# Four small moves in a TensorE-bound attention and MLP kernel: a weight transfer in halves, later numerators, two matmuls ahead of a spread, an epsilon on TensorE

## Chip, cores, metric

One core of one Trainium2 chip. The metric is the device time of one execution in microseconds (us), the median of several runs. The kernel before takes 294.08 us. The experiments ran later, in three rounds on three chips, each beside the kernel before, whose medians there were 293.73, 293.66 and 293.97; so compare ratios, and absolute times only within a round.

## The reference, cut to what matters

```python
# linear attention: 8 batches, 8 heads, 576 tokens, 64 wide; phi(x) = elu(x) + 1
q_p, k_p = phi(q), phi(k)
kv  = einsum('bhsd,bhse->bhde', k_p, v)
z   = sum(k_p, axis=2)
num = einsum('bhsd,bhde->bhse', q_p, kv)
den = einsum('bhsd,bhd->bhs', q_p, z)[..., None] + 1e-06
x   = (num / den) as 4608 tokens x 512
# two dense layers
h = x @ w_in                 # 512 x 2048
out = (h - tanh(h)) @ w_out  # 2048 x 512
```

## The kernel before

The 4608 tokens pass in nine chunks of 512. A chunk's first layer is 64 matmuls (line L366), its second layer 64 (L387), and the attention of the next batch is laid between them. During chunk 0 the weights still arrive, and batch 1 is prepared with four spare PSUM banks (`side`); PSUM is the memory that matmuls write to, and this kernel deals it out in banks of 512 columns. The attention divides a numerator (`num`) by a denominator (`den`). `num1` writes five tiles in turn into the banks that `side` hands out, directly after `a_den` has taken one, so its **fourth** tile (pair 2) falls on the bank of den. `1/den` is spread over partitions by matmuls (L240 for batch 0, L354 for batch 1), whose result VectorE multiplies with num into xT.

```python
def a_den(b, banks, parts=range(4)):
    ps = banks()[:, 0:J * 16]
    for t in range(4) if b == 0 else ():          # epsilon by TensorE, batch 0 only
        nc.tensor.matmul(ps[32 * t:32 * t + 32], eps[:, 0:32], one[:, 0:J * 16], start=True, stop=False)
    ...                                           # 16 matmuls into ps (L276)
    if b > 0:
        den = rpool.tile([128, J * 16], F32, name="den")
        nc.vector.tensor_scalar(den, ps, 1e-6, None, ALU.add)    # L281
    else:
        den = ps
    nc.vector.reciprocal(rden, den)               # L285
# cut: a_split, four VectorE operations on rden, the last one is L298
# cut: load_wo(g) loads w_out rows 512 g to 512 g + 512, one quarter

# chunk 0
side = Banks([4, 5, 6, 7])
def num1():
    sub["ns"] = new_ns(1)
    for p in (NP, 0, 1, 2, 3):
        a_num_copy(1, sub["ns"], p, side)         # matmul L320/L317, then a ScalarE copy L346/L344
s2[7].append(lambda: (a_qT_pe(1, 0, side), a_kv(1, side), a_qT_pe(1, 1, side)))
s2[8].append(lambda: b0_scale_rest(side))
s2[9].append(lambda: (a_den(1, side), num1(), a_split(1)))
s2[11].append(lambda: spread1(0))                 # L354
...
order = [((0, 0), (0, 1)), ((2, 0), (2, 1), (0, 2), (0, 3), (2, 2), (2, 3)),
         [(p, fi) for p in (1, 3) for fi in range(4)]]
for n, part_ in enumerate(order):
    if n == 1:
        open2()                                   # second spread L240, then the scalings L244
    ...
# later chunks: num of the next batch after second-layer step 11 + p (chunk 1)
s2[(11 if c == 1 else 9) + p].append(lambda p=p: a_num(n1, p))
```

Of the kernel before, what the change touches and what calls it, by code (L numbers as in the profile page):

```python
# [18 lines left out]
def kernel(  # L19
# [9 lines left out]
    nc = tc.nc  # L29
# [4 lines left out]
    NP = H // 2  # L34
# [79 lines left out]
    def load_wo(g):  # L114
        nc.gpsimd.dma_start(out=w_out_sb[:, 4 * g:4 * g + 4, :],
                            in_=moe_w_out[512 * g:512 * g + 512, :].rearrange("(ko ki) f -> ki ko f", ki=128))
# [150 lines left out]
    def a_den(b, banks, parts=range(4)):  # L267

        kz, qT = kz_t[b], qT_t[b]
        ps = banks()[:, 0:J * 16]  # L270
        for t in range(4) if b == 0 else ():
            nc.tensor.matmul(ps[32 * t:32 * t + 32], eps[:, 0:32], one[:, 0:J * 16], start=True, stop=False)
        for n, p in enumerate((0, 2, 1, 3)):
            if n in parts:
                for t in range(4):
                    nc.tensor.matmul(ps[32 * t:32 * t + 32], kz[:, p // 2, p % 2, 128:160],  # L276
                                     qT[:, p % 2, :, p // 2, 16 * t:16 * t + 16],
                                     start=(n == 0 and b > 0), stop=(n == NP - 1))
        if b > 0:
            den = rpool.tile([128, J * 16], F32, name="den")  # L280
            nc.vector.tensor_scalar(den, ps, 1e-6, None, ALU.add)  # L281
        else:
            den = ps
        rden = rpool.tile([128, J * 16], F32, name="rden")
        nc.vector.reciprocal(rden, den)  # L285
        rden_t[b] = rden
# [37 lines left out]
    def a_num(b, p):  # L324
        rdb = rdb_t[b]
        ps = num_mm(b, p, attn)
        if p < NP:
            nc.vector.tensor_mul(  # L328
                xT[:, p, S * b:S * b + 512].rearrange("p (j t c) -> p j t c", j=8, t=4),
                ps.rearrange("p j (t c) -> p j t c", t=4),  # L330
                rdb[:, p, :, 0:8, :].rearrange("p t j c -> p j t c"))
        else:
            nc.vector.tensor_mul(
                xT[:, :, S * b + 512:S * b + 576].rearrange("p a (t c) -> p a t c", t=4),
                ps[:, 0:NP, :].rearrange("p a (t c) -> p a t c", t=4), rdb[:, :, :, 8, :])
# [29 lines left out]
    def l1mm(c, fi, h, p, n):  # L365
        nc.tensor.matmul(h, w_in_sb[:, 2 * (p % 2) + p // 2, fi * 128:(fi + 1) * 128], xT[:, p, c * 512:(c + 1) * 512],  # L366
                         start=(n == 0), stop=(n == NP - 1))
# [17 lines left out]
    def l2mm(gT, o, i, f0, f1):  # L385
        for fi in range(f0, f1):
            nc.tensor.matmul(o, gT[:, fi, i * 128:(i + 1) * 128], w_out_sb[:, fi, :],  # L387
                             start=(fi == 0), stop=(fi == NF - 1))
# [30 lines left out]
        nc.gpsimd.memset(v_b[i][:, 2], 1.0)  # L419
    nc.gpsimd.memset(vp[:, :, :, 128:136], 1.0)  # L420
    load_v(1)
    load_wo(2)
    load_wo(3)

    nc.vector.memset(mask, 0.0)
# [78 lines left out]
    for c in range(NC):  # L504
        gT = gpool.tile([128, NF, 512], BF16, name="gT")
        n1, n2 = c + 1, c + 2
        s1 = {i: [] for i in range(16)}
        s2 = {i: [] for i in range(16)}
        if c == 0:
            side = Banks([4, 5, 6, 7])  # L510
            sub = {}

            def spread1(h):
                sub["bp"] = a_spread_pe(1, 4, (2 * h, 2 * h + 1))
                for p in (2 * h, 2 * h + 1):
                    a_scale(1, p, sub["ns"], sub["bp"], 144 * (p % 2))
# [4 lines that stand above are left out]
                    a_num_copy(1, sub["ns"], p, side)  # L521

            s1[11].append(lambda: a_kphi(1, 0))
            s1[13].append(lambda: a_kphi(1, 1))
            s2[3].append(lambda: a_qphi(1, 0))
            s2[4].append(lambda: (a_qphi(1, 1), load_q(2), load_k(2), load_v(2)))
            s2[0].append(prepare)
# [5 lines that stand above are left out]
            qs, ks = [], []  # L533

            def exp2(pieces, src, store, name, i):
                pieces.append(phi_pieces(2, src, store, name, i))
                pieces[i][0]()

            def rest2(f):
                f[1]()  # L540
                f[2]()

            s2[11].append(lambda: (exp2(qs, q_t, qp_t, "qp", 0), rest2(qs[0])))
            s2[12].append(lambda: exp2(qs, q_t, qp_t, "qp", 1))
            s2[13].append(lambda: (spread1(1), exp2(ks, k_t, kp_t, "kp", 0), rest2(qs[1]), a_qT_dma(2)))
            s2[14].append(lambda: rest2(ks[0]))
        elif n1 < B:
            s1[8 if c == 1 else 5].append(lambda: a_kv_cols(n1, attn))
            s1[10 if c == 1 else 8].append(lambda: (a_den(n1, attn), a_spread(n1)))
            for p in range(NP + 1):  # L550
                s2[(11 if c == 1 else 9) + p].append(lambda p=p: a_num(n1, p))
        if c == 1:
            s1[1].append(lambda: a_kphi(2, 1))
            s1[3].append(lambda: (a_vp(2, 0), a_vp(2, 1)))
        if c >= 1 and n2 < B:

            s1[0].append(lambda: (gate(qT_t[n1]), load_k(n2), load_q(n2), load_v(n2)))
            d = 2
            s2[d].append(lambda: a_kphi(n2, 0))
            s2[d + 2].append(lambda: a_kphi(n2, 1))  # L560
            s2[d + 4].append(lambda: a_qphi(n2, 0))
            s2[d + 6].append(lambda: (a_qphi(n2, 1), a_qT_dma(n2)))
            for i in range(2):
                s2[14 + i].append(lambda i=i: a_vp(n2, i))
        if c == 0:

            first = Banks([4, 5, 6, 7, 0, 1, 2, 3])
            hs = [ps_all[:, n, :] for n in range(4)]
            order = [((0, 0), (0, 1)), ((2, 0), (2, 1), (0, 2), (0, 3), (2, 2), (2, 3)),
                     [(p, fi) for p in (1, 3) for fi in range(4)]]  # L570
            seen = [0] * 4
            for n, part_ in enumerate(order):
                if n == 1:
                    open2()
                for x in range(2 if n == 0 else 0):
                    for p, fi in part_:
                        nc.tensor.matmul(hs[fi][:, 256 * x:256 * x + 256], w_in_sb[:, 0, fi * 128:(fi + 1) * 128],
                                         xT[:, p, 256 * x:256 * x + 256], start=(x == 0), stop=False)
                        seen[fi] = 1
                for p, fi in part_ if n else ():  # L580
                    l1mm(c, fi, hs[fi], p, seen[fi])
                    seen[fi] += 1
            for fi in range(4):
                l1act(fi, hs[fi], gT)
        for fi in range(4 if c == 0 else 0, NF):
            h = first() if c == 0 else dense()
            for p in range(NP):
                l1mm(c, fi, h, p, p)
            if c == 0:
                l1act(fi, h, gT)  # L590
            elif fi % 2:
                n = dense.order[(dense.n - 1) % 6]
                l1act2(fi - 1, ps_all[:, n - 1:n + 1, :], gT)
            for f in s1[fi]:
                f()
        os_ = {}
        for s in range(16):

            (g, i) = divmod(s, 4) if c == 0 else (s % 4, s // 4)
            if g == 0:  # L600
                os_[i] = ps_all[:, i, :] if c == 0 else dense()
            if c == NC - 1 and i == 3:

                if g == 0:
                    o2 = dense()
                    for o, f in ((os_[i], slice(0, 384)), (o2, slice(384, DM))):
                        for fi in range(NF):
                            nc.tensor.matmul(o[:, f], gT[:, fi, 384:512], w_out_sb[:, fi, f],
                                             start=(fi == 0), stop=(fi == NF - 1))
                        evac(c, i, o, f.start, f.stop)  # L610
                continue
            l2mm(gT, os_[i], i, 4 * g, 4 * g + 4)
            if g == 3:
                evac(c, i, os_[i])
            for f in s2[s]:
                f()
# [30 lines left out]
```

## Time and profile before

| | kernel before |
|---|---|
| time, median | 294.08 us |
| span in the trace | 291.8 us |
| TensorE busy | 97%, granted clock 1.00 throughout |
| VectorE, ScalarE busy | 60%, 48% |

How to read it: the kernel is bound by TensorE nearly everywhere, so only delays of TensorE's own starts count. The lines for three such delays are in the prediction below, with the reason why busy shares do not show them. The timeline of the kernel before has the num matmuls of batch 1 and ScalarE's copies of them:

```profile
43.36 1.03 PE L317 MATMUL ps_all<-qT,kz 128*128 128x512 bf16 x4
43.83 2.06 ACT L344 COPY ns<-ps_all 128x512 f32<-128x512 f32 x4
```

The columns of a timeline are start and duration in us, engine, line, operation, tiles, and count. Four matmuls in 1.03 us is 3 x 0.216 + 0.38: they run without any gap.

### The profile page before, as it was taken

Reading aid. Unit: us, or ns where it says so; the run is one execution under the profiler, and the core shown is the slowest. Engines: PE = TensorE matmul, PEld = TensorE weight load, DVE = VectorE, ACT = ScalarE, POOL = GpSimd, SP = SyncE. Lnnn points to the kernel's source line nnn. Section 1 sums busy time; section 2 is a strip of 40 time slices with the busy share of each in tenths; the row PEclk is TensorE's granted clock in tenths of the full one; section 3 lists DMA queues with packets and bytes.
Section 4 is the critical chain, followed back from the end, with each engine's and each line's share of the span. In section 5 each row is a group of like instructions: output and inputs, shape, how many; then the busy total and the mean of one; then the engine's idle time right before and its main releaser. Section 6 shows DMA issues by size and latency. Waiting matters only on the chain.

```text
span 291.8 us, 4476 instructions
## 1 busy us (share of the span) xinstructions
PE 284.2 (97%) x1775; PEld 134.5 (46%) x1803; DVE 174.8 (60%) x266; ACT 139.7 (48%) x168; POOL 33.1 (11%) x55
## 2 busy tenths in 40 slices
PE   8999999999999999999999999999999999999994
PEld 3544464454454444544444445444444444444443
DVE  4759958987458674776478637865581457106600
ACT  4838638846254733465345534751551155126411
POOL 8673030110030003000300030000000000000000
PEclk9999999999999999999999999999999999999999
DMA  6999999998989668955795579766117310130032
GB/s 96 198 204 212 208 207 213 214 168 145 253 158 159 170 131 135 200 139 127 134 223 131 120 137 196 144 142 139 32 34 168 73 36 0 42 84 20 0 74 72
DMA packets 39077, 38.94 MB, mean 133 GB/s; under 512 B 16336, under 2 KB 33808, under 8 KB 38288
## 3 DMA queue, kind: packets, MB, share of 16 engines
q0 software_dynamic: 17552, 18.35, 39.0%
q1 hardware_dynamic: 21344, 20.17, 30.5%
q8 instruction: 14, 0.23, 0.3%
q10 hardware_dynamic: 160, 0.13, 0.1%
q14 instruction: 7, 0.06, 0.1%
HBM read 43.91 MB, written 9.55 MB: 183 GB/s over the span
## 4 chain that ended last, share of the span: by engine, by line
PE 75%; DMA 18%; POOL 2%; issue 1%; SPq 1%; DVE 1%; ACT 1%; DVEq 0%; POOLq 0%
PE ps_all L366 37%; PE ps_all L387 32%; DMA w_out_sb<-in_moe_w_out_dram 6%; DMA w_in_sb<-in_moe_w_in_dram 3%; DMA rdb<-ds 3%; DMA out_dram<-osb 2%; PE ps_all L199 2%; DMA kraw<-in_k_dram 2%; PE ps_all L317 2%; DMA ds<-rden 1%; PE ps_all L276 1%; POOL v L419 1%; ACT osb L396 1%; SPq L401 0%; POOL qraw L90 0%
## 5 line engine op out<-in xcount | busy, mean ns | idle before, releaser
L366 PE MATMUL ps_all<-xT,w_in_sb 128*128 128x512 bf16 x558 | 126.5, 380 | 0.9 <-issue 0.2
L387 PE MATMUL ps_all<-w_out_sb,gT 128*128 128x512 bf16 x548 | 126.2, 380 | 0.7
L373 DVE TENSOR_TENSOR gT<-ps_all,th 128x1024 bf16<-128x1024 f32 x64 | 77.9, 1218 | 59.7 <-ACT th L372 59.7
L372 ACT ACTIVATE th<-ps_all 128x1024 f32<-128x1024 f32 x64 | 65.5, 1023 | 57.0 <-PE ps_all L366 46.4
L366 PEld LDWEIGHTS <-w_in_sb 128*128 128x128 bf16 x574 | 55.0, 98 | 66.0
L387 PEld LDWEIGHTS <-gT 128*128 128x128 bf16 x560 | 54.1, 98 | 64.7 <-issue 0.6
L396 ACT COPY osb<-ps_all 128x512 f32<-128x512 f32 (+1 forms) x36 | 20.8, 582 | 72.3 <-PE ps_all L387 55.9
L328 DVE TENSOR_TENSOR xT<-ps_all,rdb 128x512 bf16<-128x512 f32 x24 | 16.3, 689 | 13.7 <-PE ps_all L317 11.2
L134 ACT ACTIVATE e<-qraw 128x1152 bf16<-128x1152 bf16 x16 | 18.5, 1161 | 7.3 <-DMA qraw<-in_q_dram 7.3
L134 ACT ACTIVATE e<-kraw 128x1152 bf16<-128x1152 bf16 x15 | 17.4, 1162 | 0.1
L136 DVE TENSOR_TENSOR qp<-e,r 128x1152 bf16<-128x1152 bf16 x16 | 12.1, 758 | 7.8 <-ACT e L134 7.0
L136 DVE TENSOR_TENSOR kp<-e,r 128x1152 bf16<-128x1152 bf16 x15 | 11.4, 758 | 7.9 <-ACT e L134 7.0
L383 POOL COPY g<-qT 1x1 bf16<-1x1 bf16 x5 | 0.9, 182 | 119.7 <-DMA qT<-qp 119.7
L378 DVE TENSOR_TENSOR gT<-ps_all,th 128x512 bf16<-128x512 f32 x16 | 10.3, 686 | 2.3 <-ACT th L377 1.7
L377 ACT ACTIVATE th<-ps_all 128x512 f32<-128x512 f32 x16 | 9.2, 598 | 4.4 <-PE ps_all L366 3.2
L444 PE MATMUL ps_all<-zero 128*128 128x512 bf16 x29 | 9.3, 487 | 1.2 <-DVE zero L405 1.2
L317 PE MATMUL ps_all<-qT,kz 128*128 128x512 bf16 x28 | 10.1, 380 | 0.1
L135 DVE TENSOR_SCALAR r<-qraw 128x1152 bf16<-128x1152 bf16 x16 | 7.3, 453 | 1.9 <-DMA qraw<-in_q_dram 1.9
L199 PEld LDWEIGHTS <-kp 64*128 64x128 bf16 x216 | 6.4, 94 | 2.5 <-issue 2.5
L285 DVE RECIPROCAL rden<-den 128x144 f32<-128x144 f32 x7 | 7.4, 1052 | 0.2
L199 PE MATMUL ps_all<-vp,kp 64*128 64x136 bf16 x216 | 7.4, 220 | 0.0
L394 DVE COPY osb<-ps_all 128x128 f32<-128x128 f32 x1 | 0.3, 291 | 11.6 <-DMA out_dram<-osb 11.6
(84 smaller groups left out, 123.0 us busy)
## 6 DMA issues: line engine op xcount, KB each, us to landing
out_dram<-osb SPq DMA_DIRECT2D x70, 128.0 KB
rdb<-ds SPq DMA_DIRECT2D x12, 576.0 KB
kraw<-in_k_dram POOLq DMA_DIRECT2D x7, 576.0 KB, 7.1
qraw<-in_q_dram POOLq DMA_DIRECT2D x7, 576.0 KB, 9.2
v<-in_v_dram POOLq DMA_DIRECT2D x7, 576.0 KB, 11.9
w_out_sb<-in_moe_w_out_dram POOLq DMA_DIRECT2D x4, 512.0 KB, 16.0
w_in_sb<-in_moe_w_in_dram POOLq DMA_DIRECT2D x6, 256.0 KB, 8.6
qraw<-in_q_dram POOLq DMA_DIRECT2D x2, 288.0 KB, 4.4
```

The costliest lines, as they stand in the source:

```text
L134: return (lambda: nc.scalar.activation(e, x, AF.Exp), lambda: nc.vector.tensor_scalar(r, x, 0.0, 1.0, ALU.max, ALU.add), lambda: nc.vector ...
L136: lambda: nc.vector.tensor_tensor(y, e, r, ALU.min))
L199: nc.tensor.matmul(ps[hg][:, i, :], kp[r, i, j].rearrange("p h d -> p (h d)"), vp[r, i, j, :], start=(j == 0), stop=(j == J - 1))
L317: nc.tensor.matmul(ps, kz[:, p // 2, p % 2, 0:128], qT[:, p % 2, 0:8, p // 2, :], start=True, stop=True)
L328: nc.vector.tensor_mul(xT[:, p, S * b:S * b + 512].rearrange("p (j t c) -> p j t c", j=8, t=4), ps.rearrange("p j (t c) -> p j t c", t=4), ...
L366: nc.tensor.matmul(h, w_in_sb[:, 2 * (p % 2) + p // 2, fi * 128:(fi + 1) * 128], xT[:, p, c * 512:(c + 1) * 512], start=(n == 0), stop=(n ...
L372: nc.scalar.activation(th, h, AF.Tanh)
L373: nc.vector.tensor_sub(gT[:, fi:fi + 2, :], h, th)
L378: nc.vector.tensor_sub(gT[:, fi, :], h, th)
L387: nc.tensor.matmul(o, gT[:, fi, i * 128:(i + 1) * 128], w_out_sb[:, fi, :], start=(fi == 0), stop=(fi == NF - 1))
L396: nc.scalar.copy(osb[:, f0:f1], o[:, f0:f1])
L444: nc.tensor.matmul(ps_all[:, 0, :], zero[:, 0:128], zero, start=True, stop=True)
```

## The change

Its intent is to remove four waits: (1) for the third w_out quarter, by loading it in halves; (2) ahead of the second 1/den spread of batch 0, by laying two matmuls there; (3) for the 1/den chain of batch 1, by letting TensorE add the epsilon as it does for batch 0; (4) for the broadcast of 1/den of batch 2, by taking its num later.

```diff
 def a_den(...):
-        for t in range(4) if b == 0 else ():
+        for t in range(4) if b < 2 else ():
             nc.tensor.matmul(ps[32 * t:32 * t + 32], eps[:, 0:32], one[:, 0:J * 16], start=True, stop=False)
 ...
-                                     start=(n == 0 and b > 0), stop=(n == NP - 1))
-        if b > 0:
+                                     start=(n == 0 and b > 1), stop=(n == NP - 1))
+        if b > 1:
 ...
-    load_wo(2)
+    for n in range(2):
+        nc.gpsimd.dma_start(out=w_out_sb[:, 8 + 2 * n:10 + 2 * n, :],
+                            in_=moe_w_out[1024 + 256 * n:1280 + 256 * n, :].rearrange("(ko ki) f -> ki ko f", ki=128))
 ...
-                s2[(11 if c == 1 else 9) + p].append(lambda p=p: a_num(n1, p))
+                s2[min(12 + p, 15) if c == 1 else 9 + p].append(lambda p=p: a_num(n1, p))
 ...
-            order = [((0, 0), (0, 1)), ((2, 0), (2, 1), (0, 2), (0, 3), (2, 2), (2, 3)),
+            order = [((0, 0), (0, 1)), ((2, 0), (2, 1)), ((0, 2), (0, 3), (2, 2), (2, 3)),
                      [(p, fi) for p in (1, 3) for fi in range(4)]]
-                if n == 1:
+                if n == 2:
                     open2()
 ...
             # first layer of chunk 2: pairs 0 and 1 of its first two blocks, then pairs 2 and 3
+            if c == 2 and fi == 1:
+                for two in (0, 2):
+                    for f, o in ((0, ...), (1, h)):
+                        for p in (two, two + 1):
+                            l1mm(c, f, o, p, p)
 ...
-            l2mm(gT, os_[i], i, 4 * g, 4 * g + 4)
+            if c == 0 and g == 2:        # four blocks with the first half, then four with the second
+                for n in (2 * i, 2 * i + 1):
+                    f = 8 + 2 * (n // 4)
+                    l2mm(gT, os_[n % 4], n % 4, f, f + 2)
```

More of the change, by code (lines that the diff above doesn't have):

```diff
@@ L586 @@
             h = first() if c == 0 else dense()
-            for p in range(NP):
-                l1mm(c, fi, h, p, p)
+            if c == 2 and fi == 1:
+                for two in (0, 2):
+                    for f, o in ((0, ps_all[:, dense.order[(dense.n - 2) % 6], :]), (1, h)):
+                        for p in (two, two + 1):
+                            l1mm(c, f, o, p, p)
+            elif c != 2 or fi > 1:
+                for p in range(NP):
+                    l1mm(c, fi, h, p, p)
             if c == 0:
@@ L611 @@
                 continue
-            l2mm(gT, os_[i], i, 4 * g, 4 * g + 4)
+            if c == 0 and g == 2:
+                for n in (2 * i, 2 * i + 1):
+                    f = 8 + 2 * (n // 4)
+                    l2mm(gT, os_[n % 4], n % 4, f, f + 2)
+            else:
+                l2mm(gT, os_[i], i, 4 * g, 4 * g + 4)
             if g == 3:
```

## The prediction

> **What bounds the kernel now.** I read the page first, then the chain in order of time, then the timeline around the places that the diff touches. The page:
>
> ```profile
> PE 284.2 (97%) x1775; PEld 134.5 (46%) x1803; DVE 174.8 (60%) x266; ACT 139.7 (48%) x168; POOL 33.1 (11%) x55
> PEclk9999999999999999999999999999999999999999
> L366 PE MATMUL ps_all<-xT,w_in_sb 128*128 128x512 bf16 x558 | 126.5, 380 | 0.9 <-issue 0.2
> L387 PE MATMUL ps_all<-w_out_sb,gT 128*128 128x512 bf16 x548 | 126.2, 380 | 0.7
> ```
>
> TensorE is the bound over the whole span, at full clock. But "97% busy" hides waits: a matmul's span is 380 ns, while in a dense run the next starts 216 ns after it, so a wait of up to some 160 ns is covered by the pipeline's tail. So I work with starts, not idle time. A group of n such matmuls lasts (n-1) x 0.216 + 0.38 us; its last start is its end less 0.38. Some records are missing (both rows should have 576), which shows as a pitch of 432 ns with a weight load in its middle; I count none of those as a wait. A walk over all PE starts with this rule leaves, after the first 18 us, three real stalls, and the diff aims at each. There are no others above 0.1 us beyond the fixed 0.1 us at each change of the array's tile shape.
>
> Stall one, the third w_out quarter, in the chain in order of time and in the timeline:
>
> ```profile
> 23.05 17.84 DMA w_out_sb<-in_moe_w_out_dram
> ...
> 40.20 0.68 PE L164 MATMUL ps_all<-ident,qp 128*128 128x128 bf16 x9
> 40.93 1.02 PE L387 MATMUL ps_all<-w_out_sb,gT 128*128 128x512 bf16 x3
> ```
>
> The ninth transpose starts at 40.20 + 0.68 - 0.22 = 40.66 (one lasts 0.22), its pitch is 0.055, so L387 could start at 40.71. It starts at 40.93, just after the transfer ends at 40.89: a stall of 0.22 us.
>
> Stall two, the 1/den chain of batch 1 on VectorE:
>
> ```profile
> 41.91 1.03 PE L387 MATMUL ps_all<-w_out_sb,gT 128*128 128x512 bf16 x4
> 42.87 0.43 PE L276 MATMUL ps_all<-qT,kz 128*32 128x144 bf16 x16
> 43.35 0.31 DVE L281 TENSOR_SCALAR den<-ps_all 128x144 f32<-128x144 f32 x1 [0.82 <-PE ps_all L276]
> 43.70 1.05 DVE L285 RECIPROCAL rden<-den 128x144 f32<-128x144 f32 x1
> 44.23 1.89 PE L387 MATMUL ps_all<-w_out_sb,gT 128*128 128x512 bf16 x8
> 45.73 0.37 DVE L298 SCALAR_TENSOR_TENSOR w<-t,part,u 128x144 bf16<-128x144 bf16 x1
> 46.16 0.30 PE L354 MATMUL ps_all<-w,sel 32*128 32x144 bf16 x8
> ```
>
> The last L387 before L354 starts at 44.23 + 1.89 - 0.38 = 45.74. A change to small tiles costs 0.31 from start to start (41.91 + 1.03 - 0.38 = 42.56 to 42.87), so L354 could start at 46.05; it starts at 46.16, after L298 ends at 46.10. Stall: 0.11 us.
>
> Stall three, num of batch 2:
>
> ```profile
> 69.80 7.88 DMA rdb<-ds
> 77.80 0.70 DVE xT L328
> 78.54 0.38 PE ps_all L317
> ...
> 77.41 1.03 PE L387 MATMUL ps_all<-w_out_sb,gT 128*128 128x512 bf16 x4
> ```
>
> Num 0 to 4 alternate between two banks, so num 2 (78.54) waits until L328 has read num 0, and that waits for the broadcast that lands at 77.68. The last L387 starts at 77.41 + 1.03 - 0.38 = 78.06; num 2 could follow at 78.28. Stall: 0.27 us.
>
> **What the Trainium skill says.** "TensorE: Matmul & The Clock Gate", section "Wait — 56ns, not 53.3ns?", gives 215.7 ns between 512-column matmuls and 55.6 ns at 128 columns on a warm array; the trace agrees (216 and 55). The same page, section "The mechanism" of Part 3, says that matmuls on different 32-wide tiles run at once, some 4 ns apart; here sixteen L276 take 0.43 us in all, so it agrees. "PSUM — Partial Sum Buffer", section "PSUM bank collisions raise a hardware error", asks for guards by bank and quadrant, not by address; the trace agrees that the second spread (L240) starts only when L244 has stopped reading other columns of the same banks. "DMA: Bandwidth & Descriptors", section "Queues, rings and completion order", says that each engine consumes its ring's descriptors in order, so a first half comes before a second; no run shows this for halves yet.
>
> **The change part by part.** (1) *w_out quarter in halves.* No byte is added, one more issue on GpSimd (0.74 us for a whole quarter). It delays only the last quarter's issue, and GpSimd idles 13.8 us afterwards. In the transfer view from 20 to 50 us:
>
> ```profile
> DMA packets 5924, 6.25 MB, mean 208 GB/s; under 512 B 225, under 2 KB 5920, under 8 KB 5920
> ```
>
> A quarter of 0.52 MB takes 2.5 us, a half 1.26, so the first half should land near 40.89 - 1.26 = 39.6 and the second near 40.9. The matmuls are reordered so that the first eight use the first half alone; the second half is needed only some 2.5 us after 40.7. The stall goes: -0.22.
>
> (2) *Two matmuls of the second pair ahead of the second spread.*
>
> ```profile
> 15.64 1.35 DVE L244 TENSOR_TENSOR xT<-ns,ps_all 128x256 bf16<-128x256 f32 x3 [0.50 <-PE ps_all L240]
> 16.12 0.71 PE L577 MATMUL ps_all<-xT,w_in_sb 128*128 128x256 bf16 x4
> 17.05 0.73 PE L240 MATMUL ps_all<-rden,sel 32*128 32x128 f32 x16 [0.22 <-DVE xT L244]
> 17.70 2.70 PEld L366 LDWEIGHTS <-w_in_sb 128*128 128x128 bf16 x14
> 17.91 1.28 DVE L244 TENSOR_TENSOR xT<-ns,ps_all 128x512 bf16<-128x512 f32 x2 [0.92 <-PE ps_all L240]
> ```
>
> TensorE could go on at 16.67 (the last half-width matmul starts at 16.56 and takes 0.11) and idles until 17.05, until the third L244 ends at 16.99. The intent is to fill that gap. But the two moved matmuls read the xT rows that this same third L244 writes: in the built program the wait passes from the spread to them. So the gap stays. They run at 17.05 and 17.26, the spread then starts 0.31 after the latter (a change of tile shape that was hidden in the idle time), at 17.57, against 17.05 + 0.43 = 17.48 if the order cost nothing: +0.09. The scaling of pair 1 follows 0.52 later: 17.91 + 0.52 + 0.69 = 19.12 at its end, and the matmul that needs it can start at 19.18. TensorE's first matmul after the spread stood at 17.72 (the second weight load of L366; that matmul's record is missing, the one at 17.93 is the next). Now it stands 0.52 later and four precede pair 1: 17.72 + 0.52 + 4 x 0.216 = 19.10, so +0.07. Before, it came at 17.72 + 6 x 0.216 = 19.01 with 18.60 ready. Sum: **+0.16**, a loss.
>
> (3) *Epsilon of batch 1 by PE.* Four more small matmuls run at once: a row of four takes about 0.06 (sixteen start within 0.21), +0.06. L281 goes; the reciprocal starts 0.35 earlier less 0.06, and reads the bank directly, which batch 0 does already in 1.06 us. The chain ends 0.29 sooner, more than the 0.11 stall: -0.11. Net -0.05. The rest of the 0.29 is slack.
>
> (4) *Num of batch 2 later by one step, the last two together.* No instruction is added. Num 2 now comes four matmuls later, at about 79.15 where num 0 was read at 78.50: -0.27. The price to check is at the end, since chunk 2 of the first layer needs num 3's xT, and one vp copy (0.45) now stands ahead of its scaling. By the old clock num 3 would run at 80.20, its scaling from 80.64 to 81.33. Hence the new order of the first eight L366: pairs 0 and 1 of both blocks (80.55 to 81.41), then pair 2, then pair 3 at 81.63. It is in time by 0.25. Num 4 needs the bank of num 2 free at 80.26 and comes at 80.44. No new wait.
>
> Sum: -0.22 + 0.16 - 0.05 - 0.27 = -0.38 us on a TensorE-bound program, so nearly all of it arrives at the end: 294.08 - 0.38 = **293.7 us**.
>
> **The rivals.** (a) Part 2 works as meant, and its idle 0.38 is filled: then the sum is -0.38 - 0.16 - 0.38, or 293.2. Against it speaks that both readers wait for the same L244. (b) A new wait takes the place of the third stall: pair 3's scaling slips by more than its 0.25 of slack behind the vp copy. Then up to 0.27 is given back: 293.95. For it, VectorE's queue there is in order; against it, the sums above. (c) The w_out wait only moves: with TensorE later by 0.16 from part 2, the whole quarter would have been met at 40.87, so splitting would be worth just 0.06. That is already in the sum, since the two together are worth 0.06; if the half landed no earlier than the quarter, they would be worth 0: 293.75. (d) The transfers' timing differs from run to run, so that the two transfer stalls are typically larger or smaller than in the one trace: plus or minus 0.2.
>
> **Range and chances.** The three runs before spread over 0.43 us (293.9 to 294.33), and the effect is of that size. From (a) to (b), with some tenths for the chip: 293.2 to 294.1. Two per cent is 5.9 us, and all known stalls after the start together are 0.6: faster 0.01, same 0.98, slower 0.01.
>
> **What would show it right or wrong.** In the profile after: L387 follows the last transpose within 0.06 us (part 1); two L366 start near 17.05, the spread near 17.57, and the gap after the four half-width matmuls still ends when L244 does (part 2); L354 follows L387 by 0.31 (part 3); every L317 follows L387 by 0.22 and the first eight L366 of chunk 2 stand 0.216 apart (part 4). I am wrong if the moved L366 start well before 17.0, if a gap above 0.1 us appears near 81 us, or if the sum of start delays does not match the change in span.

## The result, and the profile after

The changed kernel takes 293.85 us (median of five runs, 293.51 to 294.21). The ratio to the kernel before is 0.9997, with a 95% interval of 0.9982 to 1.0011: no difference that the runs can tell.

The page after, in the lines that answer to those of before:

```profile
PE 286.1 (98%) x1807; PEld 134.7 (46%) x1807; DVE 174.7 (60%) x265; ACT 139.7 (48%) x168; POOL 33.7 (12%) x56
L387 PE MATMUL ps_all<-w_out_sb,gT 128*128 128x512 bf16 x560 | 127.5, 379 | 0.0
```

TensorE's busy time rose by 1.9 us while the span stayed, but that is no added work: 1807 matmul records stand here, only 1775 before, and the change adds four. The weight loads, 1803 before and 1807 after, differ by just these four: 28 matmul records are missing before and none after. So again the starts decide. The three stalls of before are gone or changed. The timeline after, at the second spread of batch 0 (part 2):

```profile
15.98 0.71 PE L580 MATMUL ps_all<-xT,w_in_sb 128*128 128x256 bf16 x4
16.90 0.59 PE L366 MATMUL ps_all<-xT,w_in_sb 128*128 128x512 bf16 x2 [0.22 <-DVE xT L244]
17.43 0.73 PE L240 MATMUL ps_all<-rden,sel 32*128 32x128 f32 x16
18.29 1.29 DVE L244 TENSOR_TENSOR xT<-ns,ps_all 128x512 bf16<-128x512 f32 x2 [1.44 <-PE ps_all L240]
```

The last half-width matmul (256 columns, L577 before, L580 after) starts at 15.98 + 0.71 - 0.27 = 16.42. The two moved L366 follow at 16.90, 0.49 later by the unrounded starts; before, it was the spread that followed, after the same 0.49. The gap is not filled, the wait has only passed to the moved matmuls.

The timeline after, around the transposes, den and num of batch 1 (parts 1 and 3):

```profile
40.21 0.68 PE L164 MATMUL ps_all<-ident,qp 128*128 128x128 bf16 x9
40.72 1.03 PE L387 MATMUL ps_all<-w_out_sb,gT 128*128 128x512 bf16 x4
42.73 0.42 PE L276 MATMUL ps_all<-qT,kz 128*32 128x144 bf16 x16
43.21 1.06 DVE L285 RECIPROCAL rden<-ps_all 128x144 f32<-128x144 f32 x1 [0.88 <-PE ps_all L276]
43.22 0.59 PE L317 MATMUL ps_all<-qT,kz 128*128 128x512 bf16 x2
44.32 0.59 PE L317 MATMUL ps_all<-qT,kz 128*128 128x512 bf16 x2 [0.51 <-DVE rden L285]
44.75 1.89 PE L387 MATMUL ps_all<-w_out_sb,gT 128*128 128x512 bf16 x8
45.25 0.37 DVE L298 SCALAR_TENSOR_TENSOR w<-t,part,u 128x144 bf16<-128x144 bf16 x1
46.57 0.30 PE L354 MATMUL ps_all<-w,sel 32*128 32x144 bf16 x8
```

L387 now follows the last transpose at once (40.67 to 40.72): part 1 worked. But the four num matmuls no longer run together. Two run, then TensorE stands still until the reciprocal ends at 43.21 + 1.06 = 44.27. The second pair could have started at 43.22 + 2 x 0.216 = 43.65 and starts at 44.32: a **new stall of 0.67 us**. The chain of splits ends at 45.62, nearly a microsecond ahead of L354: its gain is not used.

And at num of batch 2 (part 4):

```profile
78.69 1.03 PE L387 MATMUL ps_all<-w_out_sb,gT 128*128 128x512 bf16 x4
79.56 0.38 PE L317 MATMUL ps_all<-qT,kz 128*128 128x512 bf16 x1
80.97 4.26 PE L366 MATMUL ps_all<-xT,w_in_sb 128*128 128x512 bf16 x19
```

Num 2 follows the last L387 (78.69 + 1.03 - 0.38 = 79.34) after 0.22, and no gap stands in the matmuls of chunk 2.

To compare runs in spite of an uneven start, I measured five stretches from start to start in each trace: **A** from the last half-width matmul to the first L387; **T** from the first transpose of batch 1 to the last; **C** from there to the next L387; **D** from there to the first L354; **E** from the first key-value matmul (L199) of chunk 1 to that of chunk 2. The stretches between are the same in all traces within 0.02 us, with one exception named below. "Sum" is from the last half-width matmul to the first key-value matmul of chunk 2.

| kernel | A | T | C | D | E | sum |
|---|---|---|---|---|---|---|
| before | 14.54 | 2.65 | 0.28 | 5.22 | 28.03 | 69.53 |
| changed | 14.70 | 2.65 | 0.06 | 5.85 | 27.76 | 69.83 |

The parts so cost +0.16 (A), -0.22 (C), +0.63 (D) and -0.27 (E): together +0.30 us in place of the predicted -0.38. The span shows +0.2, because this execution started 0.14 us earlier. Either is inside the noise of the runs.

### The profile page after: what moved, and what is told of

It reads as the page before. It is cut to its first block, busy times and chain, and to the rows that moved or that the text cites. A ratio compares the mean times of both kernels' runs of the same rounds, so it can differ in the third digit from the quotient of the medians. Undisturbed runs are those within 1.5% of the kernel's fastest.

```text
span 292.0 us, 4512 instructions
## 1 busy us (share of the span) xinstructions
PE 286.1 (98%) x1807; PEld 134.7 (46%) x1807; DVE 174.7 (60%) x265; ACT 139.7 (48%) x168; POOL 33.7 (12%) x56
## 4 chain that ended last, share of the span: by engine, by line
PE 97%; DVE 1%; issue 0%; DVEq 0%
PE ps_all L366 43%; PE ps_all L387 41%; PE ps_all L447 3%; PE ps_all L199 2%; PE ps_all L317 2%; PE ps_all L618 1%; PE ps_all L276 1%; PE ps_all L164 1%; PE ps_all L177 1%; PE ps_all L240 0%; DVE xT L244 0%; PE ps_all L221 0%; DVE rden L285 0%; PE ps_all L320 0%; PE ps_all L210 0%; PE ps_all L231 0%
## 5 line engine op out<-in xcount | busy, mean ns | idle before, releaser
L366 PE MATMUL ps_all<-xT,w_in_sb 128*128 128x512 bf16 x574 | 127.7, 379 | 0.2 <-DVE xT L244 0.2
L387 PE MATMUL ps_all<-w_out_sb,gT 128*128 128x512 bf16 x560 | 127.5, 379 | 0.0
L366 PEld LDWEIGHTS <-w_in_sb 128*128 128x128 bf16 x574 | 55.0, 98 | 66.2 <-issue 0.6
L387 PEld LDWEIGHTS <-gT 128*128 128x128 bf16 x560 | 54.2, 98 | 64.2
L328 DVE TENSOR_TENSOR xT<-ps_all,rdb 128x512 bf16<-128x512 f32 x24 | 16.5, 691 | 13.7 <-PE ps_all L317 11.4
L199 PEld LDWEIGHTS <-kp 64*128 64x128 bf16 x216 | 6.4, 94 | 2.5 <-issue 2.5
L199 PE MATMUL ps_all<-vp,kp 64*128 64x136 bf16 x216 | 7.4, 220 | 0.0
L135 DVE TENSOR_SCALAR r<-kraw 128x1152 bf16<-128x1152 bf16 x15 | 6.8, 451 | 0.0
```

The costliest lines, as they stand in the source:

```text
L135: lambda: nc.vector.tensor_scalar(r, x, 0.0, 1.0, ALU.max, ALU.add),
L199: nc.tensor.matmul(ps[hg][:, i, :], kp[r, i, j].rearrange("p h d -> p (h d)"), vp[r, i, j, :], start=(j == 0), stop=(j == J - 1))
L328: nc.vector.tensor_mul(xT[:, p, S * b:S * b + 512].rearrange("p (j t c) -> p j t c", j=8, t=4), ps.rearrange("p j (t c) -> p j t c", t=4), ...
L366: nc.tensor.matmul(h, w_in_sb[:, 2 * (p % 2) + p // 2, fi * 128:(fi + 1) * 128], xT[:, p, c * 512:(c + 1) * 512], start=(n == 0), stop=(n ...
L387: nc.tensor.matmul(o, gT[:, fi, i * 128:(i + 1) * 128], w_out_sb[:, fi, :], start=(fi == 0), stop=(fi == NF - 1))
```

## The experiments

All kernels gave correct results. **Theory:** the reciprocal of batch 1 now reads the den bank itself and holds it for 1.06 us, where L281 had released it after 0.31; the fourth num matmul needs that bank and waits. **Rivals:** TensorE only arrived earlier than something else; or it waits for the 1/den chain as such, wherever it stands.

### Part 3 undone

```diff
-        for t in range(4) if b < 2 else ():
+        for t in range(4) if b == 0 else ():
 ... (both tests on b > 1 back to b > 0)
```

> The changed kernel with part 3 alone undone (the epsilon of batch 1 is added by VectorE again). My theory: in the changed kernel the reciprocal reads the den bank directly and holds it for 1.06 us, where the short add had released it after 0.31, and the fourth num matmul of batch 1, which is to write that same bank, waits: 0.67 us of stall, against 0.11 us that the earlier epsilon won at the first spread and 0.07 us for the four added matmuls. So here the five num matmuls stand 0.216 us apart or closer, the 0.1 us wait before the first spread is back, and from the first den matmul to the first spread of batch 1 it takes 3.29 us (as in the kernel before) in place of 3.84. Time: 0.55 us under the changed kernel, 293.3. Rival (the stall comes from something else that the change moved, the earlier arrival of TensorE by 0.2 us or ScalarE's copies): the stall of 0.67 stays and the time is as the changed kernel's, 293.85.

Measured: 293.77 us, ratio to before 0.9993 (0.9980 to 1.0007). The timeline:

```profile
43.78 0.31 DVE L281 TENSOR_SCALAR den<-ps_all 128x144 f32<-128x144 f32 x1 [0.82 <-PE ps_all L276]
43.79 1.03 PE L317 MATMUL ps_all<-qT,kz 128*128 128x512 bf16 x4
```

The four num matmuls run together again, and D is 5.22 as before. The stall belongs to part 3. The sum of the stretches is 69.20, 0.33 under before, which is what the prediction's other three terms add up to. The time went down less than the 0.55 I expected, and its interval cannot tell.

### Num of pairs 2 and 3 four matmuls later

```diff
-                for p in (NP, 0, 1, 2, 3):
+                for p in (NP, 0, 1):
                     a_num_copy(1, sub["ns"], p, side)
+            s2[10].append(num1b)          # num1b: pairs 2 and 3
```

> The changed kernel, with num of pairs 2 and 3 of batch 1 four second-layer matmuls later, nothing else. My theory (the bank is held by the reciprocal until 44.27): the fourth num matmul now comes 0.86 us later, when the bank is free, so no stall at num; the chain of splits ends at 45.62, well ahead of the first spread, so no wait there either. From the first den matmul to the first spread: 3.17 us (3.84 less 0.67). Time 293.2. Rival (TensorE waits for the 1/den chain as such, whatever it does meanwhile): the wait moves to the first spread and the time stays at 293.85.

Measured: 293.68 us, ratio 0.9993 (0.9980 to 1.0005). The stall at num is gone. D is 5.33, not the 5.18 that my 3.17 meant (it leaves out the 2.01 ahead of den): a wait of 0.15 us stands before the first spread. It is not the rival's wait for the chain, as the timeline shows:

```profile
45.37 1.07 ACT L344 COPY ns<-ps_all 128x512 f32<-128x512 f32 x2 [0.16 <-PE ps_all L317]
45.69 0.37 DVE L298 SCALAR_TENSOR_TENSOR w<-t,part,u 128x144 bf16<-128x144 bf16 x1
46.49 0.31 PE L354 MATMUL ps_all<-w,sel 32*128 32x144 bf16 x8
```

The chain ends at 46.06, ScalarE's last copy at 46.44, and the spread starts 0.05 after the latter. It writes all four side banks, and the copy is still reading one. My expectation had overlooked that the later num delays the copies too.

### Part 3 alone

The edit is part 3 of the diff, put on the kernel before.

> The kernel before with part 3 alone. My theory: the stall of about 0.67 us at the fourth num matmul appears here too, the wait of 0.1 us at the first spread goes, four matmuls cost 0.07: from the first den matmul to the first spread 3.84 us in place of 3.29. Time 0.5 to 0.6 us over the kernel before, 294.6. Rival (it needs the other parts, which bring TensorE there sooner): no stall, time as before, 294.08.

Measured: 294.48 us against 293.73, ratio 1.0020 (1.0008 to 1.0033): slower by 0.6 us, as expected, and clear of noise. D is 5.84. The part harms by itself, without the others.

### A den bank that num does not use

```diff
                 sub["ns"] = new_ns(1)
+                three = Banks([side.order[(side.n + i) % 4] for i in range(3)])
                 for p in (NP, 0, 1, 2, 3):
-                    a_num_copy(1, sub["ns"], p, side)
+                    a_num_copy(1, sub["ns"], p, three)
+                side.n += 5
```

> The changed kernel with one difference: the five num tiles of batch 1 go round the three banks that den does not use, so that none waits for the reciprocal. My theory: the fourth num matmul now waits for ScalarE's copy of the first num tile (ends at about 43.8 by the changed kernel's clock) and the fifth for the copy of the second (about 44.2), so the stall shrinks from 0.67 to about 0.4 us in two pieces and ends with ScalarE's copies as releasers, not the reciprocal. Time about 0.25 us under the changed kernel, 293.6. Rival (the stall is the reciprocal's result, not its bank): unchanged 0.67 with VectorE as releaser.

Measured: 293.92 us, ratio 1.0001 (0.9988 to 1.0013). The timeline:

```profile
43.10 1.06 DVE L285 RECIPROCAL rden<-ps_all 128x144 f32<-128x144 f32 x1 [0.88 <-PE ps_all L276]
43.11 1.49 PE L317 MATMUL ps_all<-qT,kz 128*128 128x512 bf16 x4
43.31 0.37 ACT L346 COPY ns<-ps_all 128x256 f32<-128x256 f32 x1 [2.02 <-PE ps_all L320]
```

The reciprocal lasts until 44.16, yet the third of these matmuls starts at 43.73, right after ScalarE's copy ends at 43.68, and the fourth at 44.22. So TensorE does not need the reciprocal's result here; it needed its bank. The stall shrinks from 0.67 to 0.46 us (0.19 and 0.27), in two pieces as expected and somewhat longer than the 0.4; D is 5.64. The time does not resolve the 0.2.

### Part 2 undone

```diff
-            order = [((0, 0), (0, 1)), ((2, 0), (2, 1)), ((0, 2), (0, 3), (2, 2), (2, 3)),
+            order = [((0, 0), (0, 1)), ((2, 0), (2, 1), (0, 2), (0, 3), (2, 2), (2, 3)),
-                if n == 2:
+                if n == 1:
```

> The changed kernel with part 2 alone undone (the second 1/den spread directly after the four half-width matmuls, as before). My theory: the moved matmuls wait for the same VectorE scaling as the spread, so the move fills nothing and costs 0.16 us: from the last half-width matmul to the first second-layer matmul it takes 14.54 us as in the kernel before, in place of 14.70. Time 0.1 to 0.2 us under the changed kernel, 293.7, within its noise. Rival (the move fills part of the idle 0.38 us, as it was meant to): the stretch grows over 14.70 and the time by 0.2 or more.

Measured: 293.75 us, ratio 0.9998 (0.9985 to 1.0011). A is 14.54, as the theory has it; but T is 2.78 instead of 2.65, and the sum, 69.80, is 0.03 under the changed kernel's. What A gave, another wait took: the key-value matmuls of batch 1 now wait for v, which is still arriving. In this execution part 2's 0.16 us would have hidden that; in others v came in time without it (T is 2.65 in the kernel before and 2.66 in a later kernel without part 2).

### Part 1 undone

The edit puts `load_wo(2)` and the old order of the second-layer matmuls back.

> The changed kernel with part 1 alone undone (the third w_out quarter in one transfer, its matmuls in the old order). My theory: the quarter lands near 40.9 us, the second-layer matmul could start near 40.72, so 0.1 to 0.25 us of stall after the last transpose of batch 1 (0.28 us from start to start before, 0.055 in the changed kernel). Since the start of the kernel and the landing vary from run to run by 0.1 to 0.2 us, the size is uncertain. Time up to 0.2 us over the changed kernel, 294.0. Rival (the stall is the change from transposes to matmuls or ScalarE): distance as in the changed kernel, 0.055.

Measured: 294.34 us against 293.66, ratio 1.0018 (1.0006 to 1.0030). C is 0.39: a stall of 0.33, larger than I expected, since in this execution the quarter landed only at 41.39. The three traces with the whole quarter have stalls of 0.22 (before), 0.38 (part 3 alone) and 0.33 (here, beside part 2, where my rival (c) gave it 0.06), so the halves are worth 0.2 to 0.4 us.

### Part 4 undone

The edit puts the old `s2` line and the plain loop over the blocks of chunk 2 back.

> The changed kernel with part 4 alone undone (num of batch 2 one step earlier each, old order of the first eight matmuls of chunk 2). My theory: num 2 of batch 2 waits 0.27 us for the scaling of num 0, which waits for the broadcast of 1/den, as in the kernel before: between the second-layer layers of chunk 1 and the first key-value matmul of chunk 2 the stretch from the first key-value matmul of chunk 1 to that of chunk 2 takes 28.03 us in place of 27.76. Time 0.27 us over the changed kernel, 294.1. Rival (in the changed kernel the broadcast would have come in time anyway): 27.76 and no wait.

Measured: 294.15 us, ratio 1.0014 (1.0001 to 1.0027). The timeline:

```profile
78.82 1.03 PE L387 MATMUL ps_all<-w_out_sb,gT 128*128 128x512 bf16 x4
79.07 1.89 DVE L328 TENSOR_TENSOR xT<-ps_all,rdb 128x512 bf16<-128x512 f32 x3 [2.36 <-PE ps_all L317]
79.82 0.38 PE L317 MATMUL ps_all<-qT,kz 128*128 128x512 bf16 x1
```

From 79.47 to 79.82 is 0.35, so the stall is 0.13 and E is 27.89. The wait is there, but half as long as before: L328 started 1.54 us after num 0 here and 1.68 in the kernel before. In the third trace with the old order (part 3 alone) the stall was 0.19. So this wait varies from execution to execution with the broadcast's arrival, and 0.27 was its upper end. This kernel's span of 293.1 is also some 0.7 longer than the others of its round for another reason: its second half of q came late, and its last half-width matmul started at 17.41.

### The parts that paid, without the stall

Part 2 undone, and num of pairs 2 and 3 later.

> The parts that paid, with the stall of part 3 removed: the changed kernel with part 2 undone and num of pairs 2 and 3 of batch 1 four matmuls later. My theory: 0.16 and 0.67 us under the changed kernel's trace (span about 291.2 us at its start) and about 0.55 under the kernel before: 293.2 to 293.5, ratio 0.998. Rival (the moved waits turn up elsewhere): a ratio of 1.000 and a new wait in its trace.

Measured: 293.35 us, ratio 0.9987 (0.9975 to 0.9999). A 14.54, D 5.33, E 27.76, sum 69.16: 0.37 us under before, a little less than the half microsecond expected, because of the same wait for ScalarE's last copy.

### Parts 1 and 4 only

> Parts 1 and 4 only: the changed kernel with part 2 and part 3 undone. My theory, that the four parts add up stage by stage: the old 14.54 us from the last half-width matmul to the first second-layer one, 3.28 us from the first den matmul to the first spread of batch 1 (with its old wait of 0.1), no w_out wait, 27.76 us between the key-value products of chunks 1 and 2. From the last half-width matmul to the end 274.85 us against 275.29 for the kernel before, 275.60 for the changed one and 274.93 for the best so far. Time 293.3. Rival (parts depend on each other; without part 2 TensorE is back at the w_out quarter earlier and waits for its first half, or for v): 275.0 to 275.2 with a wait named in the trace.

Measured: 293.44 us against 293.97, ratio 0.9981 (0.9967 to 0.9995). The sum is 69.30, 0.23 more than expected; for most of that the rival gave the right reason. In the chain of waits:

```profile
22.42 16.27 DMA v<-in_v_dram
...
38.74 1.66 PE ps_all L177 x36
```

The transfer of v ends at 38.70 and the key-value matmuls start at 38.74; T is 2.79. Another 0.10 us stand in the first layer of chunk 1, at 51.6, the exception announced above; what it waited for I did not settle.

### Num after three matmuls

The base is the kernel of "The parts that paid, without the stall" (part 2 undone); `num1b` moves from `s2[10]` to here:

```diff
                 for n in (2 * i, 2 * i + 1):
                     f = 8 + 2 * (n // 4)
-                    l2mm(gT, os_[n % 4], n % 4, f, f + 2)
+                    l2mm(gT, os_[n % 4], n % 4, f, f + 1)
+                    if n == 5:
+                        num1b()
+                    l2mm(gT, os_[n % 4], n % 4, f + 1, f + 2)
```

> The best so far with num of pairs 2 and 3 of batch 1 after three instead of four second-layer matmuls. My theory: in the best so far the first spread still waits 0.15 us, now for ScalarE's copy of the last num tile (ended 46.09, spread at 46.14), because num came 0.86 us later than it had to for the bank; one matmul earlier lets that copy end some 0.15 to 0.2 us sooner, while the bank is free at 44.36. So from the first den matmul to the first spread 3.17 us in place of 3.32, and from the last half-width matmul to the end 274.78. Time 293.2. Rival (the copies were not what was waited for): 3.32 stays.

Measured: 293.40 us against 293.97, ratio 0.9976 (0.9964 to 0.9989), faster than the kernel before, and faster than the changed kernel, which took 294.21 in the same round (below). From parts 1 and 4 only, 293.44 in the same round, the time cannot tell it. The timeline:

```profile
44.06 2.12 ACT L344 COPY ns<-ps_all 128x512 f32<-128x512 f32 x4
45.12 1.24 PE L387 MATMUL ps_all<-w_out_sb,gT 128*128 128x512 bf16 x5
46.29 0.30 PE L354 MATMUL ps_all<-w,sel 32*128 32x144 bf16 x8
```

The copies end at 46.18; the spread follows the last L387 (45.12 + 1.24 - 0.38 = 45.98) after 0.31, which is the plain change of tile shape. D is 5.20 and the sum 69.07, 0.46 under before and the lowest of all. But D without part 3 is 5.22: freed of its stall, part 3 is worth just 0.02 us, and the rest of the lead over parts 1 and 4 only is the wait for v (T) and the 0.10 at 51.6, which this execution had less of or not at all.

### The changed kernel again

> The changed kernel once more, unaltered, for the comparison on the same chip and for a second trace. My theory: the fourth num matmul of batch 1 stalls 0.67 us again and the first spread follows the first den matmul after 3.84 us; the stages are as in its first trace within 0.02 us, other than the start (first 16.4 us), which varied by 1.2 us over the traces so far. Time 293.7 to 294.1. Rival (that stall was a chance of one execution): it is absent or of another length.

Measured: 294.21 us against 293.97, ratio 1.0005 (0.9990 to 1.0020). A 14.70, C 0.06, D 5.85, E 27.76, sum 69.83, each as in the first trace. The stall is no chance of one execution.

The three kernels that end clear of noise on the slow side lack part 1, lack part 4, or have part 3 without the gains; the three clear on the fast side have parts 1 and 4 and no stall at num. Part 3 undone (sum 69.20) and num of pairs 2 and 3 later (69.31) have that too, but their times are not clear. Each interval is a 95% one, and those of "part 4 undone" and "parts that paid" miss 1 by only 0.0001, so for single kernels the stretches are the better evidence:

| kernel | A | T | C | D | E | sum | ratio to before |
|---|---|---|---|---|---|---|---|
| part 3 alone | 14.54 | 2.79 | 0.44 | 5.84 | 27.95 | 70.38 | 1.0020 |
| part 1 undone | 14.70 | 2.65 | 0.39 | 5.84 | 27.77 | 70.16 | 1.0018 |
| part 4 undone | 14.70 | 2.65 | 0.06 | 5.85 | 27.89 | 69.96 | 1.0014 |
| parts that paid | 14.54 | 2.66 | 0.06 | 5.33 | 27.76 | 69.16 | 0.9987 |
| parts 1 and 4 | 14.54 | 2.79 | 0.06 | 5.22 | 27.76 | 69.30 | 0.9981 |
| num after three | 14.54 | 2.70 | 0.06 | 5.20 | 27.76 | 69.07 | 0.9976 |

## Why the prediction was right or wrong

The time, 293.85, lies in the range, and "same" was right. The sum behind it was not: -0.38 was predicted, and the stretches show +0.30. That the time came so close to 293.7 is luck of the noise: measured again in the last round, the changed kernel took 294.21, above the range and 0.24 over the kernel before.

- **Part 1, -0.22: right** (C from 0.28 to 0.06). The first half landed at 39.77 and the second at 41.02, against the 39.6 and 40.9 worked out. The remark that it would be worth 0.06 beside part 2 rests on a landing at 40.89; in the one trace of that kind the quarter landed at 41.39, and the whole transfer cost 0.33.
- **Part 2, +0.16: right within its stretch** (A from 14.54 to 14.70, in all traces with it), and so was the reason, that the moved matmuls wait for the same L244. Missing was that v is on its way there too: without part 2, TensorE waits for v instead, between 0 and 0.15 us depending on the execution, so undoing it gained only 0.03 in the trace.
- **Part 3, -0.05: this step failed.** "The chain ends 0.29 sooner, more than the 0.11 stall: -0.11 ... The rest of the 0.29 is slack." The four matmuls cost 0.08 and the stall at the spread went, as said; even the sign that I named for this part, 0.31 from L387 to L354, came true. But I followed the chain only forward, to who waits for its result, and not to who waits for the bank that L281 had read. Measured: +0.63, made of a stall of 0.67 at the fourth num matmul, plus the 0.08, less the 0.11, rounded. With the stall removed, D falls by 0.02 (5.22 to 5.20), not by 0.05.
- **Part 4, -0.27: right in the trace compared**, with no new wait; in other executions the removed wait was 0.13 and 0.19, so on average it is worth less.
- **The rivals:** (a) and (b) did not occur: the moved matmuls start 0.49 after the last half-width one, as the spread did, and no gap stands near 81 us. (d) did: the waits for w_out, v and the broadcast differ by 0.1 to 0.2 us between executions.
- **A reading:** "both rows should have 576" is wrong. The weight loads of L366 number 574 and those of L387 560, before and after; it changes nothing in the sum.

That the wrong term did not carry the time out of the range is due to its size: an error of 0.68 us is a quarter of a per cent, and the runs of one kernel spread over nearly a microsecond. Part of that spread is the start: over the thirteen traces the last half-width matmul started anywhere from 16.25 to 17.41.

## What to carry to other kernels

Before removing a short operation that copies a PSUM tile, ask who waits for the bank and not only who waits for the values: a cheap operation in front of a slow one may be what frees the bank. When TensorE is bound and the gains are tenths of a microsecond, compare stretches between fixed matmuls in the traces, since whole times drown them. And a wait that is removed early in a kernel that still loads may only bring TensorE sooner to the next transfer.

## What the Trainium skill lacked or had wrong

- "PSUM — Partial Sum Buffer", section "PSUM bank collisions raise a hardware error", asks for guards by bank and quadrant; this kernel agrees, as the second spread starts at 17.05, just after L244 has stopped, at 16.99, reading other columns of the same banks. (Num also overwrites den's own columns, so the stall at num alone cannot tell a bank from an address.) The section does not say what follows for the choice of the reader: an operation holds the bank for its whole duration, here 1.06 us for a reciprocal of 128x144 from PSUM and 0.31 for an add of the same size, and the difference became 0.67 us of TensorE stall.
- "VectorE: DVE Perf Modes", section "First, the fixed hardware budget", says that the reciprocal is an iterative divide, but no page gives its time: 1.05 us for 144 columns from SBUF and 1.06 from PSUM, against 0.31 for the add.
- "TensorEngine Tiling (Array Packing)", section "Key Properties", says that changing the tiling mode drains TensorE, without a figure: here it is 0.09 us, 0.31 from start to start in place of 0.216, at L387 to L276 and at L387 to L354.
- "DMA: Bandwidth & Descriptors", section "Anatomy of one DMA — SWDGE (gpsimd) path", gives about 2 us of fixed cost for one transfer, and does not say that transfers queued behind each other need not pay it one after the other: in the changed kernel the two halves of a quarter landed 1.25 us apart, half of the 2.54 us of the whole quarter behind them.
- No page says that matmul records can be missing: 1775 of them stand in the trace before and 1807 after, where the program has four more, and the second trace of the changed kernel has 1778.
